# Three-operator kernel on one core: the mixer's second product in halves through the projections' bank, a later round for the second group, and another order at the end of the last batch

## The chip, the cores and the metric

The kernel runs on one core of a Trainium2 chip. The metric is the device time of one execution in microseconds (us), less is better. On the core, TensorE (PE) multiplies matrices, VectorE (DVE), ScalarE (ACT) and GpSimd (POOL) work on vectors, and SyncE (SP) issues the DMA transfers; each engine takes its instructions strictly in the order in which they stand in its own queue. TensorE writes into PSUM, a memory of 8 banks of 512 fp32 elements on each of 128 partitions.

## The reference, cut to what matters

Three operators follow one another on a batch of B = 4 sequences of S = 768 positions with 512 features. The third is the one whose second product the change touches.

```python
# 1: attention in chunks of 32 with a context of 16 to the left and 8 to the right (8 heads of 64)
a = softmax(scale * q_chunk @ k_context.T);  x = a @ v_context
# 2: causal attention with E = 4 experts as heads (width 64), two chosen per position
logits = x @ w_gate                     # the two best, softmax -> w
for e in range(E):
    a = softmax(causal(scale * (x @ wq[e]) @ (x @ wk[e]).T))
    out += w[e] * (a @ (x @ wv[e]) @ wo[e])
# 3: mixer along the positions (rank 32), then two layers (512 -> 2048 -> 512)
h = (x.transpose(0, 2, 1) @ U) @ V
u = x + h.transpose(0, 2, 1)
return u + np.maximum(u @ w_ch1, 0.0) @ w_ch2
```

## The kernel before

The program has two phases. In the first, each batch goes through twelve rounds; round r treats one pair of experts (`pr`, two pairs) and one block of 128 positions (`i`, six blocks), so that rounds 0 to 11 cover a batch. A round (`rnd`, line 700) writes down, in this order: the scores and softmax of its own block (`scores`), the chunk attention of a unit of the next batch (`local_scores`, `local_turn`), a list `fill1`, the transposes of the previous round's probabilities (`turn_scores`), a list `fill2`, and then, as one unbroken run on TensorE, the products with the values (`values`) and, where asked, the mixer's first product (`mix_down`). The lists carry the projections of later halves (`qk_proj`, `v_proj`) and the mixer's other steps. In the second phase TensorE runs the two layers over all batches (`ph` and `po`, lines 294 and 310, and `acc`, line 990).

A scheduler lays out each engine's queue from the written order, the dependencies and its own estimates, while the order of writing alone decides which buffer a tile gets. So a moved line can change the queues of whole batches. No table of order was written by hand; the rounds in which pieces stand are fixed in the loop of lines 821 to 861.

The names that matter below. `sc` is a block's scores in PSUM, `nmc` the negative maximum over a row (line 606, VectorE), `ac` the exponentials (line 591, ScalarE), `su` the sums and their reciprocals (lines 610 and 611, VectorE). Line 613 scales `ac` in place by `su` and the gate on GpSimd. `tpc` are the transposes of `ac` (line 631); line 634 copies them from PSUM to `ath`, in turn on ScalarE and VectorE. `t` takes the products (line 696), and line 649 copies a block of the result into `yT`, which holds 128 features by 768 positions of one pair. Once a pair has its six blocks, the mixer works on it: `mix_turn` transposes `yT` (`pyt`, line 659) and copies it to `y` (lines 661 and 662); `mix_down` multiplies by U (six small matmuls out of `y` and `u_s`, line 696); `mix_keep` sums the pieces into `qf` and `qm` (lines 673 to 679); `mix_up` multiplies by V (`pz`, line 687), adds `yT` (`z`, line 688, one VectorE instruction of 768 columns), and sends `z` to memory (`zs`, line 689), from where the second phase loads it (`zf`).

PSUM is shared by tags. `TC` has two buffers of two banks each, which `sc`, `tpc`, `pyt` and `pz` take in turn. `TQ` is one bank with one buffer; the projections `pqk` (line 499, 384 columns wide) and `pv` (line 539) live in it, in the last batch also the second layer's `po`. A tile can be written only when the one that held its buffer before has been read out.

`mix_up` of a batch's first pair stands at the head of `fill1` in round 0 of the next batch, that of the second pair in round 4. The last batch has no next one: after its twelve rounds comes an extra round that has no block of its own, with `mix_up(b, 0)` in its `fill1`, and then the second pair's `mix_turn`, `mix_down`, `mix_keep` and `mix_up`.

## Time and profile before

| what | us |
|---|---|
| three runs, least | 845.24 |
| three runs, median | 845.29 |
| three runs, most | 847.5 |
| the profiled execution, its own time | 846.73 |
| its span, from the first instruction to the last | 844.7 |
| TensorE busy in the span | 804.9 (95%) |
| VectorE busy | 625.0 (74%) |
| ScalarE busy | 498.0 (59%) |
| GpSimd busy | 155.8 (18%) |

Between the span and the execution's own time lie 2.03 us that no view shows. A busy TensorE means that a matmul was under way, not that it ran at its peak. A row of the timeline gives the start, the duration, the engine, the line, the operation and its operands, and in square brackets how long the engine sat idle before it and whose end released it; a row with xN merges N instructions that followed one another. A row of the stretches ("windows") gives the length, each engine's busy time, the clock that was granted to TensorE as a share of its full speed, and the DMA's share. Since queues are in order, an idle time in front of an instruction holds up all that stands behind it on the same engine.

### The profile page before, as it was taken

What the parts mean: (1) busy time and instruction counts of PE and PEld (TensorE: products, weight loads), DVE (VectorE), ACT (ScalarE), POOL (GpSimd) and SP (SyncE); (2) the same over time, 40 slices, a digit from 0 to 9 for tenths busy, and PEclk for the clock granted to TensorE, in tenths of its full rate; (3) what the DMA queues carried; (4) which work ended last, traced back from release to release, by engine and by line L of the source; (5) the groups of instructions that cost most, each with busy time, mean ns of one, the idle gap of its engine ahead of it and who ended that gap; (6) DMA issues with size and microseconds to landing.
All of it is one profiled execution on the core that took longest, in us unless ns stands there. A gap on an engine that the chain in (4) does not pass through costs nothing.

```text
span 844.7 us, 17957 instructions
## 1 busy us (share of the span) xinstructions
PE 804.9 (95%) x6396; PEld 721.1 (85%) x6396; DVE 625.0 (74%) x1990; ACT 498.0 (59%) x1464; POOL 155.8 (18%) x243
## 2 busy tenths in 40 slices
PE   7889999999998998889979999999999999999997
PEld 5768989889987897768767888899999999999996
DVE  4597768677767766899536999999769486684956
ACT  5688757667656755666424565666555464554642
POOL 1364344344333424223110000000000000000000
PEclk9999999999999999999979999999999999999999
DMA  9845323333313301263206744300303012030211
GB/s 289 256 137 155 100 81 104 91 123 109 94 54 95 95 2 45 87 191 104 75 19 204 222 155 163 101 26 1 125 1 126 1 45 81 1 125 2 76 50 51
DMA packets 38377, 81.54 MB, mean 97 GB/s; under 512 B 4368, under 2 KB 7952, under 8 KB 37520
## 3 DMA queue, kind: packets, MB, share of 16 engines
q1 hardware_dynamic: 38288, 80.39, 29.6%
q8 instruction: 51, 0.84, 0.4%
q14 instruction: 38, 0.31, 0.1%
HBM read 64.64 MB, written 15.73 MB: 95 GB/s over the span
## 4 chain that ended last, share of the span: by engine, by line
PE 71%; DMA 11%; DVE 10%; ACT 5%; issue 3%; SPq 0%; POOL 0%; DVEq 0%; ACTq 0%; POOLq 0%
PE acc L990 23%; PE ph L294 13%; PE t L696 8%; PE pqk L499 6%; DMA raw<-in_w 5%; PE tpc L631 3%; PE pv L539 3%; PE po L310 3%; PE s L440 3%; PE sc L579 3%; PE sc L580 2%; DMA part<-o 2%; PE tp L468 2%; ACT ac L591 1%; DMA k_t<-in_kw 1%
## 5 line engine op out<-in xcount | busy, mean ns | idle before, releaser
L990 PE MATMUL acc<-xhi,sw 128*128 128x256 f32 x1008 | 189.2, 283 | 0.4 <-ACT o L315 0.3
L990 PEld LDWEIGHTS acc<-xhi,sw 128*128 128x128 f32 x1008 | 159.7, 189 | 5.5 <-ACT o L315 0.5
L990 PE MATMUL acc<-xlo,sw 128*128 128x256 f32 x504 | 139.4, 283 | 0.2 <-DVE xlo L909 0.2
L905 DVE TENSOR_TENSOR sx<-t 128x256 f32<-128x256 f32 x180 | 68.1, 422 | 66.8 <-ACT t L898 66.8
L898 ACT ACTIVATE t<-ph 128x512 f32<-128x512 f32 x72 | 43.0, 598 | 99.0 <-PE ph L294 99.0
L613 POOL TENSOR_SCALAR ac<-ac,su,g 128x128 f32<-128x128 f32 (+5 forms) x96 | 71.4, 752 | 147.5 <-DVE su L611 95.2
L990 PEld LDWEIGHTS acc<-xlo,sw 128*128 128x128 f32 x504 | 95.6, 190 | 2.4 <-DVE xlo L909 0.4
L908 ACT CAST xhi<-sx 128x256 fp32r<-128x256 f32 x205 | 74.6, 406 | 21.8 <-DVE sx L905 18.9
L591 ACT ACTIVATE ac<-sc,nmc 128x128 f32<-128x128 f32 (+5 forms) x96 | 60.3, 632 | 38.3 <-DVE nmc L606 26.8
L909 DVE TENSOR_TENSOR xlo<-sx,xhi 128x256 fp32r<-128x256 f32 x205 | 77.5, 422 | 2.8 <-ACT xhi L908 2.0
L447 ACT ACTIVATE a<-a,nm 128x96 f32<-128x96 f32 x192 | 69.9, 368 | 12.7 <-DVE nm L444 12.2
L294 PE MATMUL ph<-zh,wp_l 128*128 128x512 f32 x192 | 61.0, 398 | 1.0 <-ACT zh L282 1.0
L294 PE MATMUL ph<-zh,wp_h 128*128 128x512 f32 x192 | 60.9, 394 | 0.0
L631 PE MATMUL tpc<-ident_s,ac 128*128 128x128 f32 x336 | 53.9, 281 | 6.5 <-ACT ath L634 2.8
L452 POOL TENSOR_TENSOR a<-a,rs 128x288 f32<-128x288 f32 x64 | 42.6, 667 | 91.8 <-DVE rs L451 32.9
L440 PE MATMUL s<-k_t,q_t 128*128 128x96 f32 x384 | 54.0, 275 | 4.3 <-DVE nm L444 1.6
L294 PE MATMUL ph<-zl,wp_h 128*128 128x512 f32 x176 | 56.1, 394 | 0.0
L440 PEld LDWEIGHTS s<-k_t,q_t 128*128 128x128 f32 x384 | 48.9, 192 | 7.7 <-DVE nm L444 3.6
L579 PE MATMUL sc<-kl,qs 128*128 128x384 f32 (+2 forms) x144 | 51.0, 355 | 3.8 <-DVE z L688 1.0
L444 DVE CUSTOM_DVE_ANT_0 a<-s,band_s 128x96 f32<-128x96 f32 x192 | 40.1, 251 | 16.8 <-PE s L440 14.3
L696 PE MATMUL t<-ath,vt 128*64 128x128 f32 x672 | 47.1, 280 | 4.3 <-DVE ath L634 3.7
L631 PEld LDWEIGHTS tpc<-ident_s,ac 128*128 128x128 f32 x336 | 39.9, 145 | 12.2 <-issue 4.6
(183 smaller groups left out, 1975.1 us busy)
## 6 DMA issues: line engine op xcount, KB each, us to landing
raw<-in_w SPq DMA_DIRECT2D x64, 256.0 KB, 3.5
q_t<-in_qT SPq DMA_DIRECT2D x32, 384.0 KB, 3.3
k_t<-in_kw SPq DMA_DIRECT2D x32, 288.0 KB, 3.8
v_t<-in_vw SPq DMA_DIRECT2D x32, 288.0 KB, 3.2
part<-o SPq DMA_DIRECT2D x24, 256.0 KB, 2.5
pt<-part SPq DMA_DIRECT2D x6, 1024.0 KB, 5.0
out<-pt SPq DMA_DIRECT2D x24, 256.0 KB, 2.3
zf<-zs SPq DMA_DIRECT2D x8, 512.0 KB, 4.5
```

Of the source, the lines that this page charges most:

```text
L294: nc.tensor.matmul(p, w[f // 4][:, pr, fs], z[:, pr], start=(n == 0), stop=(n == 5))
L440: last = nc.tensor.matmul(s[:, j, :], w["q"][:, qd * 3 + j], w["k"][:, qd * 3 + j], start=True, stop=True).ins
L447: nc.scalar.activation(a[:, j, :], a[:, j, :], AF.Exp, bias=nm[:, j:j + 1], scale=-1.0, accum_out=ss[:, j:j + 1])
L579: nc.tensor.matmul(s[:, o:o + w], q, kl[b, e, hf][:, :w], start=True, stop=False)
L591: nc.scalar.activation(aa[h][:, :n], src, AF.Exp, bias=nm[:, h:h + 1], scale=1.0, accum_out=su[:, h:h + 1])
L613: nc.gpsimd.tensor_scalar(aa[h][:, :n], aa[h][:, :n], su[:, h:h + 1], gates[b, i // 3][:, i % 3, 2 * pr + h:2 * pr + h + 1], op0=ALU.mult, ...
L631: nc.tensor.transpose(tp[h][:, j * 128:(j + 1) * 128], aa[h][:, j * 128:(j + 1) * 128], ident_s)
L696: session.append(nc.tensor.matmul(*a, **kw).ins)
L905: nc.vector.tensor_tensor(x, t[:, p[0], p[1]], t[:, q[0], q[1]], op=op)
L908: nc.scalar.copy(hi, x)
L909: nc.vector.tensor_sub(lo, x, f32(hi))
L990: ended[0] = nc.tensor.matmul(acc[n][:, m], w[:, ms], x, start=(f == FA and u == 0 and m == 0), stop=(f == NF - 2 and u == 2 and m == 1)).ins
```

## The change

Four things are changed.

- In five of the eight calls of `mix_up` (both pairs of batches 0 and 1 and the first pair of batch 2) the product goes through `TQ` in two halves: one matmul of 384 columns into the one bank, one add of 384 columns out of it, then the same for the other half. The three other calls keep the two banks of `TC` and the one add of 768 columns.
- The second pair's `mix_up` stands in round 5 of the next batch, not in round 4.
- In the last batch's extra round `mix_up(b, 0)` is taken out of `fill1` and stands behind the second pair's `mix_turn`.
- From round 10 of the last batch on, line 613's scalings are issued on VectorE, not on GpSimd. These are four instructions: two of 640 columns and two of 768.

```diff
--- before.py
+++ after.py
@@ -610,10 +610,12 @@
             nc.vector.tensor_scalar(su, su, 1e-9, None, op0=ALU.add)
             nc.vector.reciprocal(su, su)
             for h in range(2):
-                nc.gpsimd.tensor_scalar(aa[h][:, :n], aa[h][:, :n], su[:, h:h + 1],
-                                        gates[b, i // 3][:, i % 3, 2 * pr + h:2 * pr + h + 1], op0=ALU.mult, op1=ALU.mult)
+                (nc.vector if ending[0] else nc.gpsimd).tensor_scalar(
+                    aa[h][:, :n], aa[h][:, :n], su[:, h:h + 1], gates[b, i // 3][:, i % 3, 2 * pr + h:2 * pr + h + 1],
+                    op0=ALU.mult, op1=ALU.mult)
             a_ts[b, pr, i] = aa
 
+        ending = [False]
         ncp = [0]
         turned_ins = []
 
@@ -681,11 +683,18 @@
         def mix_up(b, pr):
             qm = qms.pop((b, pr))
             z = cw.tile([128, S], F32, name="z", tag="ac", bufs=NAC)
-            p = ps.tile([128, 1024], F32, name="pz", **TC)
-            for hf in range(2):
-                cs = slice(128 + hf * HALF, 128 + (hf + 1) * HALF)
-                nc.tensor.matmul(p[:, cs], qm, v_st[:, hf * HALF:(hf + 1) * HALF], start=True, stop=True)
-            nc.vector.tensor_add(z, p[:, 128:128 + S], yT[b, pr])
+            if b < B - 2 or (b, pr) == (B - 2, 0):
+                for hf in range(2):
+                    cs = slice(hf * HALF, (hf + 1) * HALF)
+                    p = ps.tile([128, 512], F32, name="pz", **(TQ))[:, :HALF]
+                    nc.tensor.matmul(p, qm, v_st[:, cs], start=True, stop=True)
+                    nc.vector.tensor_add(z[:, cs], p, yT[b, pr][:, cs])
+            else:
+                p = ps.tile([128, 1024], F32, name="pz", **TC)
+                for hf in range(2):
+                    cs = slice(128 + hf * HALF, 128 + (hf + 1) * HALF)
+                    nc.tensor.matmul(p[:, cs], qm, v_st[:, hf * HALF:(hf + 1) * HALF], start=True, stop=True)
+                nc.vector.tensor_add(z, p[:, 128:128 + S], yT[b, pr])
             nc.sync.dma_start(zs[b][:, pr, :], z)
 
         session = []
@@ -821,11 +830,12 @@
             work = pieces(b, 1) + ([] if last else pieces(b + 1, 0))
             for r, (pr, i) in enumerate(ROUNDS):
                 n = (FILL0 if b == 0 else FILL)[r] if work else 0
+                ending[0] = last and r >= 10
                 now, work = work[:n], work[n:]
                 f1, f2 = now[:1], now[1:]
                 if b and r == 1:
                     f2 = f2 + [lambda: mix_turn(b - 1, 1)]
-                if b and r == 4:
+                if b and r == 5:
                     f1 = [lambda: mix_up(b - 1, 1)] + f1
                 if r == 10:
                     f2 = f2 + [lambda: mix_turn(b, 0)]
@@ -851,8 +861,9 @@
                     if r == 5:
                         close_proj()
             if last:
-                rnd(None, old, fill1=[lambda: mix_up(b, 0)])
+                rnd(None, old)
                 mix_turn(b, 1)
+                mix_up(b, 0)
                 session.clear()
                 pq = ps.tile([128, 512], F32, name="pq", **TE)
                 mix_down(b, 1, pq)
```

How this moves instructions, at three places. The first is TensorE's queue at the start of batch 1 (round 0, after the mixer's first product for batch 0, `pq`); `tp` and `s` belong to the chunk attention. Before:

```order
L696 MATMUL pq<-y,u_s 32x128 x6
L468 MATMUL tp<-ident_s,a 96x128 x6
L499 MATMUL pqk<-xl,wqk_h 128x384 x4
L499 MATMUL pqk<-xh,wqk_h 128x384 x4
L499 MATMUL pqk<-xh,wqk_l 128x384 x4
L440 MATMUL s<-k_t,q_t 128x96 x3
L687 MATMUL pz<-v_st,qm 128x384 x2
L631 MATMUL tpc<-ident_s,ac 128x128 x6
L440 MATMUL s<-k_t,q_t 128x96 x3
L631 MATMUL tpc<-ident_s,ac 128x128 x6
```

Now, beginning at the same round's products with the values (the rows between, which stand behind the same `pq`, are twelve `tpc`, six `tp` and the next scores):

```order
L440 MATMUL s<-k_t,q_t 128x96 x3
L705 MATMUL t<-ath,vt 64x128 x12
L690 MATMUL pz<-v_st,qm 128x384
L633 MATMUL tpc<-ident_s,ac 128x128
L440 MATMUL s<-k_t,q_t 128x96 x3
L690 MATMUL pz<-v_st,qm 128x384
L661 MATMUL pyt<-ident_s,yT 128x128 x6
L633 MATMUL tpc<-ident_s,ac 128x128
L440 MATMUL s<-k_t,q_t 128x96 x3
L499 MATMUL pqk<-xl,wqk_h 128x384 x4
L499 MATMUL pqk<-xh,wqk_h 128x384 x4
L499 MATMUL pqk<-xh,wqk_l 128x384 x4
```

The group of twelve `pqk` that stood ahead of `pz` stands behind both halves of `pz` now, and the next scores and the transposes of `yT` (`pyt`) have come ahead of it; the pieces of projection behind it stand later too, about a round, through the batches 1 to 3.

The second place is TensorE's queue at the end of the last batch, from the last scores to the first product of the second phase (`ph`). Before:

```order
L582 MATMUL sc<-tri_s,identb_s 128x128
L631 MATMUL tpc<-ident_s,ac 128x128 x10
L696 MATMUL t<-ath,vt 64x128 x10
L696 MATMUL t<-y,u_s 32x128 x6
L687 MATMUL pz<-v_st,qm 128x384 x2
L631 MATMUL tpc<-ident_s,ac 128x128 x12
L659 MATMUL pyt<-ident_s,yT 128x128 x5
L696 MATMUL t<-ath,vt 64x128 x12
L659 MATMUL pyt<-ident_s,yT 128x128
L294 MATMUL ph<-zh,wp_l_5571 128x512 x2
```

Now:

```order
L582 MATMUL sc<-tri_s,identb_s 128x128
L633 MATMUL tpc<-ident_s,ac 128x128 x16
L705 MATMUL t<-ath,vt 64x128 x10
L705 MATMUL t<-y,u_s 32x128 x6
L633 MATMUL tpc<-ident_s,ac 128x128 x6
L661 MATMUL pyt<-ident_s,yT 128x128 x5
L705 MATMUL t<-ath,vt 64x128 x12
L696 MATMUL pz<-v_st,qm 128x384 x2
L661 MATMUL pyt<-ident_s,yT 128x128
L294 MATMUL ph<-zh,wp_l_5581 128x512 x2
```

Six of the twelve transposes of the last block have moved ahead of the products with the values, the other six ahead of `pyt`, and `pz` has moved from ahead of them to behind the last products; from the first `ph` on the queue reads as before. (The trace counts two matmuls for each of the products `t<-ath` and `t<-y` of these rows: x20 there is x10 here.)

The third is VectorE's queue over the same stretch, from the last maxima to the second copy of `y`. Before:

```order
L606 TENSOR_REDUCE nmc<-sc 128x1 x2
L610 TENSOR_SCALAR su<-su 128x2
L611 RECIPROCAL su<-su 128x2
L634 COPY ath<-tpc 128x640
L675 TENSOR_TENSOR qf<-t,qf 32x128
L678 CAST qm<-qf 32x128
L679 TENSOR_TENSOR qm<-qf,qm 32x128
L688 TENSOR_TENSOR z<-pz,yT 128x768
L634 COPY ath<-tpc 128x768
L662 COPY y<-pyt 128x256
```

Now, from the last sums on:

```order
L610 TENSOR_SCALAR su<-su 128x2
L611 RECIPROCAL su<-su 128x2
L613 TENSOR_SCALAR ac<-ac,su,g 128x768 x2
L636 COPY ath<-tpc 128x640
L677 TENSOR_TENSOR qf<-t,qf 32x128
L636 COPY ath<-tpc 128x768
L680 CAST qm<-qf 32x128
L681 TENSOR_TENSOR qm<-qf,qm 32x128
L697 TENSOR_TENSOR z<-pz,yT 128x768
L664 COPY y<-pyt 128x256
```

The two scalings of 768 columns have come in behind the sums, and `z` has moved behind the last copy `ath` and the steps of `qm`. The two scalings of 640 columns, not shown, stand one round earlier, ahead of the last maxima.

## Rows read from the trace of the kernel before

**Rows 1.** The stretches: length, busy PE, PEld, DVE, ACT, POOL, granted clock, DMA share, GB/s.

```profile
150.00:350.00 200.00, 191.26 (x1920) 174.38 (x1920) 142.79 (x525) 128.58 (x439) 75.75 (x120) 1.00 0.25 79
350.00:370.00 20.00, 14.65 (x96) 11.45 (x95) 18.11 (x61) 12.82 (x38) 4.44 (x8) 1.00 0.54 165
450.00:845.00 395.00, 388.50 (x2575) 355.94 (x2573) 308.48 (x808) 213.92 (x518) 0.00 (x0) 1.00 0.24 82
```

**Rows 2.** TensorE's waits in 150 to 340: in total, times, longest, in us.

```profile
PE t L696 <- DVE ath L634: 2.5, 5, 0.9
...
PE tpc L631 <- DVE z L688: 1.1, 2, 0.6
...
PE tpc L631 <- ACT ath L634: 0.8, 2, 0.4
PE sc L579 <- DVE z L688: 0.7, 2, 0.5
```

**Rows 3.** One line's instructions over the span: duration min/median/max in ns, starts, forms.

```profile
L687 PE MATMUL pz<-v_st,qm x16: 335/379/657, 150.2 to 445.9; 96*128 96x384 f32 x16
...
L688 DVE TENSOR_TENSOR z<-pz,yT x8: 936/955/958, 151.5 to 446.8; 128x768 f32<-128x768 f32 x8
...
L487 DVE TENSOR_TENSOR xl<-t,xh x32: 526/554/560, 18.5 to 319.4; 128x384 fp32r<-128x384 f32 x32
...
L130 DVE TENSOR_SCALAR d_t<-d_t x41: 258/290/503, 37.7 to 498.4; 128x256 uint32<-128x256 uint32 x40, 128x192 uint32<-128x192 uint32 x1
```

**Rows 4.** The stretch of one batch, instructions on `pqk` alone, then on `pv` alone.

```profile
241.00:329.00 88.00, 20.73 (x101) 17.28 (x102) 8.83 (x16) 7.64 (x16) 1.00 0.19 57
...
241.00:329.00 88.00, 10.35 (x72) 9.12 (x72) 0.93 (x6) 2.23 (x6) 1.00 0.19 57
```

**Rows 5.** TensorE's longest wait in 354 to 370.

```profile
PE t L696 <- DVE ath L634: 2.1, 1, 2.1
```

**Rows 6.** The timeline at the end of the first phase, rows left out between.

```profile
425.43 1.62 PE L631 MATMUL tpc<-ident_s,ac 128*128 128x128 f32 x10 [1.40 <-ACT ac L591]
...
426.40 0.17 DVE L611 RECIPROCAL su<-su 128x2 f32<-128x2 f32 x1
426.74 1.94 POOL L613 TENSOR_SCALAR ac<-ac,su,g 128x768 f32<-128x768 f32 x2 [3.58 <-DVE su L611]
427.08 0.82 DVE L634 COPY ath<-tpc 128x640 f32<-128x640 f32 x1 [0.52 <-PE tpc L631]
...
428.05 2.40 PE L696 MATMUL t<-ath,vt 128*64 128x128 f32 x20 [1.01 <-DVE ath L634]
...
433.45 0.98 PE L687 MATMUL pz<-v_st,qm 96*128 96x384 f32 x2 [1.57 <-DVE qm L679]
...
437.19 0.96 DVE L634 COPY ath<-tpc 128x768 f32<-128x768 f32 x1 [1.70 <-PE tpc L631]
...
438.20 1.53 PE L696 MATMUL t<-ath,vt 128*64 128x128 f32 x24 [0.25 <-DVE ath L634]
...
440.10 0.33 PE L659 MATMUL pyt<-ident_s,yT 128*128 128x128 f32 x1 [0.36 <-ACT yT L649]
```

**Rows 7.** Stretches around the end and one hole earlier, columns as in the first group.

```profile
427.00:438.00 11.00, 8.37 (x52) 6.83 (x51) 3.37 (x6) 1.51 (x4) 1.68 (x2) 0.53 0.10 37
428.00:437.00 9.00, 7.38 (x47) 6.12 (x48) 1.74 (x4) 1.51 (x4) 0.68 (x1) 0.50 0.08 32
355.00:356.00 1.00, 0.00 (x0) 0.00 (x0) 1.00 (x6) 0.84 (x4) 0.13 (x1) 1.00 0.00 0
```

**Rows 8.** TensorE's timeline at the start of batch 1, rows left out between.

```profile
144.19 1.27 PE L696 MATMUL t<-ath,vt 128*64 128x128 f32 x20
145.38 0.85 PE L696 MATMUL pq<-y,u_s 128*32 128x128 f32 x12
...
150.63 0.82 PE L631 MATMUL tpc<-ident_s,ac 128*128 128x128 f32 x6
...
156.74 1.53 PE L696 MATMUL t<-ath,vt 128*64 128x128 f32 x24
```

## The prediction

> **What bounds the kernel now.** I read the stretches first. TensorE is busy for 191.26 of the 200 us from 150 to 350, and for 388.50 of the 395 us of the second phase [rows 1]: in both it is the bound, and only its idle time can be won there. Two places stand out. From 350 to 370 it is busy for 14.65 of 20 us while VectorE is busy for 18.11 [rows 1], the longest wait being 2.1 us for a copy `ath` on VectorE [rows 5]. And at the end of the first phase it waits in a chain and runs at a lower clock: in the 11 us from 427 to 438 the mean granted clock is 0.53, in 428 to 437 it is 0.50, which is the level of 1.2 GHz instead of 2.4 [rows 7]. If the clock has these two levels, (1 - 0.53) / 0.5 x 11 = 10.3 us were spent at the lower one. The chain itself is in the timeline [rows 6]: the last scalings end on GpSimd at 428.68, yet the queue puts the first product `pz` ahead of the transposes of what they scale, `pz` waits for `qm` until 433.45, and only then come the transposes, the copy, the products at 438.20 and the last `pyt` at 440.10. The last wait of this chain is `pz`'s, not the scaling's.
>
> Next, TensorE's waits in the middle of the batches [rows 2]: behind `mix_up` it waited 1.1 + 0.7 = 1.8 us for `z` to give back one of the two big buffers, and 0.8 us for copies by ScalarE that were late for the same buffers. Against these stand 2.5 us of waits for copies by VectorE, which the change doesn't aim at.
>
> **The first mixer edit, halves.** It removes the big buffer from five calls. The waits that can go are those 1.8 + 0.8 = 2.6 us; none need go if the next `tpc` is late for another reason, so 0 to 2.6. I take 2.6, as `z` or the copies that shared its buffers are named as the releaser in each of them.
>
> It adds a wait. Both halves go through one bank, so the second matmul waits until the first half's add has read it. A matmul takes 0.38 us, an add of 384 columns 0.55 (the row of line 487 has this shape), one of 768 columns 0.955 [rows 3]. The cycle until the bank is free is thus 0.93 us plus what the add waits in VectorE's queue. In the new queue only one transpose, or one and three small score products, stand between the halves. A transpose is 0.82 / 6 = 0.14 us [rows 8]. So between nothing (the scheduler's neighbours fill it) and 0.9 per call; I take 0.4, the middle, and 2.0 for five calls, with 0 to 4.5 for the range. Behind the second `pz` in TensorE's queue stand transposes and then the twelve `pqk`, and all wait with it.
>
> Two adds of 384 cost VectorE 2 x 0.554 = 1.11 us instead of 0.955 [rows 3], 0.15 more a call, 0.8 in all. VectorE is busy for 142.79 of 200 us there [rows 1], so this lies in its idle time; where a copy `ath` stands right behind, it costs up to 0.15 each. I take nothing.
>
> The row shows the fixed part of 0.15 us that an instruction pays whatever its width. The Trainium skill, "VectorE: DVE Perf Modes", section "The TRN2 errata — SBUF-src ops pay a fixed extra latency per instruction", says that many small tiles pay a fixed cost each and advises wide ones, which speaks against splitting the add. This trace agrees, with 0.15 us. With all five on the path the sum would be 0.8 worse.
>
> **What the queues do with it.** The new use of the bank moves the pieces of projection about a round later through batches 1 to 3, since the projections take the same single bank. No work is added by that, so in batches 1 and 2, where TensorE is the bound, it gives nothing on balance: some waits close, others open. I take 0 with 2.5 either way, as large as the waits for `ath` [rows 2]. The later round for the second pair's `mix_up` costs and gains nothing by itself: no engine wants its `z` within the batch, only the transfer to memory, whose queue (SP) has nothing behind it there that is due.
>
> In batch 3 the moved pieces can fall into the hole of 20 - 14.65 = 5.35 us [rows 1]. But VectorE is the late one there, and two `pqk` bring it 2 x 8.83 / 8 = 2.2 us of evictions [rows 4]. So from -4 (they fill the hole) to +2.2 (they lengthen VectorE's line); I take 0, since work moves, but none goes away.
>
> **The end.** Here the rows carry a sum. The sums `su` end at 426.57, and GpSimd begins at 426.74 and needs 1.94 for both halves [rows 6]. On VectorE one scaling of 768 columns takes between 0.55 and 0.955. The upper end is the one-element pace of the 768-wide add. The lower comes from a scalar operation of the same kind out of and into SBUF, 0.29 us for 256 columns: with the fixed 0.15 that is 0.54 ns a column, half of the add's (0.955 - 0.554) / 384 = 1.04, and 0.15 + 768 x 0.53 gives 0.55 [rows 3]. I take 0.55, the same kind of instruction. The transposes of the previous block end at 427.05. Those of the last block's first expert then begin at 426.57 + 0.55 = 427.1, end at 427.95; the second scaling ends at 427.7 and the copy `ath` of 640 columns (0.82), which stands behind it on VectorE now, at 428.5 instead of 427.90. That is what the scalings cost: the first products begin 0.5 later than before. At full clock they take 1.27, the mixer's first product 0.85, six transposes 0.82, five `pyt` 0.7, the last products 1.53 [rows 8]. So: products to 429.8, mixer to 430.6, second expert's transposes to 431.4, `pyt` to 432.1. The copy of 768 (0.96) begins at 431.5, ends at 432.5, the last products run from 432.6 to 434.1. The steps of `qm` on VectorE follow that copy and end around 433.1, beside the products. `pz` takes two matmuls, 0.5, and the last `pyt` ends at 435.1 at the latest, against 440.43 before: -5.3. With the slow scaling price 0.8 less, -4.5. What then stands behind, `ph`, has the same queue as before, and in the second phase TensorE is the bound, so this carries through to the end. The two scalings of 640 columns come earlier, ahead of the last maxima, in a stretch in which VectorE is idle before those maxima; I take them as free.
>
> Some 3 of the 5.3 us are the clock and not the order: the waits that made TensorE idle for 1.01 and 1.57 us [rows 6] go, and with them, I expect, most of the stretch at 1.2 GHz.
>
> **Sum.** -2.6 + 2.0 + 0 + 0 - 5.3 = -5.9. Against the profiled execution's own 846.73 that gives 840.8, against the runs' median of 845.29 it gives 839.4. The profile was longer than the median by 1.44, and a stretch of low clock of another length would explain that, in which case the median has less to win. I take 840.0, which puts the kernel before at 845.9 by this reckoning. By the bounds alone the sum runs from -14 to +5, but they don't all fall on one side.
>
> **Rivals.**
> The clock falls all the same. Before it fell TensorE had been idle for 1.40, transposed for 1.62, and been idle for 1.01 us [rows 6]; the 1.40 stays, since the exponentials release the transposes. Against it: around 355 TensorE stood still for a whole microsecond, 2.1 in all, at a granted clock of 1.00 [rows 5, 7]. If it falls in the same place for the same 10 us, the new chain takes about twice the prices above until the clock rises near 437.6: transposes to 428.7, products (2.40 [rows 6]) to 431.1, mixer to 432.8, transposes to 434.4, `pyt` to 435.8, the last products begin there and end near 438.3, `pz` and `pyt` around 439. That is a gain of 1.5: 845.9 - 0.6 - 1.5 = 843.8. The Trainium skill, "TensorE: Matmul & The Clock Gate", section "HAM oscillation — how this bites in real kernels", says that idle gaps between short bursts of matmuls bring the clock down again each time. The fall at 427 is of this sort, the hole at 355 speaks against it.
>
> The halves stall more than I think, 0.9 a call: 2.5 worse, 842.5.
>
> The moved pieces fill batch 3's hole: 4 better, 836.0.
>
> The projections' bank becomes the bound, and the kernel gets slower. A half then holds the bank for 0.38 + 0.55 us and about 0.4 of waiting for VectorE (waits there average 2.5 / 5 = 0.5 [rows 2]), 1.35 each and 2.7 a call, and the projections behind wait for all of it: 5 x 2.7 = 13.5, less 2.6 and 5.3, is +5.6, or 851.5. It decides where the bank has less than two calls' 5.4 us of free time in a batch. The instructions on `pqk` and `pv` take 20.73 + 8.83 + 7.64 + 10.35 + 0.93 + 2.23 = 50.7 of 88 us, counted one after the other [rows 4], which leaves 37 less what evictions wait; so this is unlikely.
>
> **Chances.** The forecast, with a short fall of the clock among it (up to 842), 0.52; the clock falls as before (843.8) 0.15; the halves stall (842.5) 0.10; the hole filled (836.0) 0.10; the bank bound (851.5) 0.08; mixtures 0.05. The range of 836.5 to 844.2 leaves out the last rival and the far end of the filled hole. A measurement tells some 0.3% from no change, 2.5 us, so faster means under 842.8 and slower over 847.8. Faster: 0.52 + 0.10 + half of the stalls + some of the mixtures = 0.70; slower 0.08; the rest, 0.22, is the same.
>
> **What would show it.** Right: behind `pz` no wait of TensorE for `z` in batches 1 and 2; the two 768-wide scalings on VectorE at 0.55 each; the last `pyt` some 5 us earlier relative to the last scores; a granted clock of 1.00 in most of that stretch. Wrong: a second `pz` that waits near a microsecond, `pqk` waiting for a half's add, scalings at 0.95, a clock of 0.50 for ten microseconds, or a second phase that gives the gain back in waits for `zh` or weights.

## Result and the profile after

The changed kernel takes 840.32 us (median of ten runs, 837.64 to 844.53). In the same comparison the kernel before takes 847.38 (845.24 to 850.35), 2.1 more than the median of the three runs known ahead. The ratio is 0.9909, interval 0.9888 to 0.9931: 0.9% faster. The forecast was 840.0 in a range of 836.5 to 844.2.

The profiled execution has a span of 838.5 us against 844.7. Its first line of busy times:

```profile
PE 803.5 (96%) x6396; PEld 720.8 (86%) x6396; DVE 631.1 (75%) x1999; ACT 497.5 (59%) x1464; POOL 152.7 (18%) x239
```

TensorE is busy for nearly as long as before (804.9) in a shorter span: idle time went, not work.

To see where, the span is cut at four points that every version has in the same order on TensorE: the mixer's first product (`y` by U) of batch 0's first pair, that of batch 2's first pair, the last scores `sc`, and the first `ph` behind the last `pyt`. Of the kernel before, the three stretches between them (the columns are length, then busy PE, PEld, DVE, ACT, POOL, granted clock, DMA share, GB/s):

```profile
145.38:327.37 181.99, 173.93 (x1768) 158.74 (x1767) 128.74 (x490) 118.38 (x407) 69.49 (x110) 1.00 0.27 82
327.37:423.79 96.42, 89.20 (x623) 74.36 (x621) 76.88 (x202) 55.38 (x148) 25.90 (x34) 1.00 0.32 105
423.79:440.18 16.39, 11.65 (x88) 9.36 (x88) 5.13 (x10) 4.34 (x10) 1.94 (x2) 0.69 0.07 25
```

And of the changed kernel:

```profile
147.68:322.85 175.17, 170.12 (x1756) 156.18 (x1754) 128.09 (x491) 117.28 (x405) 69.71 (x108) 1.00 0.28 85
322.85:422.13 99.28, 93.01 (x636) 77.68 (x634) 81.87 (x208) 55.96 (x150) 24.65 (x34) 0.98 0.31 102
422.13:433.07 10.94, 8.02 (x88) 6.32 (x88) 5.34 (x11) 4.31 (x10) 0.00 (x0) 1.00 0.01 1
```

The length less the busy PE is TensorE's idle time: 8.06, 7.22 and 4.74 us before, 5.05, 6.27 and 2.92 after. The first two stretches belong together, since the change moves projections from the first into the second (busy 173.93 to 170.12, 89.20 to 93.01). The differences of the traces, then: up to the first point +2.30 (147.68 - 145.38, work that the change doesn't touch), the middle 274.45 - 278.41 = -3.96, the end 10.94 - 16.39 = -5.45, the second phase (838.5 - 433.07) - (844.7 - 440.18) = +0.91. Sum -6.20, the difference of the spans. Of the +2.30, TensorE's busy time makes 1.89 (132.77 to 134.66 us, 1304 matmuls in both), with the clock low for 3.4 us between 40 and 50 us, where it was 1.00 before; its waits there for loads of `k_t` were shorter, 0.9 instead of 1.5.

The end of the changed kernel, rows left out between, to be read against [rows 6]:

```profile
423.67 1.65 PE L633 MATMUL tpc<-ident_s,ac 128*128 128x128 f32 x10 [1.31 <-ACT ac L591]
...
425.00 1.27 DVE L613 TENSOR_SCALAR ac<-ac,su,g 128x768 f32<-128x768 f32 x2
...
425.83 0.85 PE L633 MATMUL tpc<-ident_s,ac 128*128 128x128 f32 x6 [0.52 <-DVE ac L613]
426.19 0.82 DVE L636 COPY ath<-tpc 128x640 f32<-128x640 f32 x1
...
427.06 1.31 PE L705 MATMUL t<-ath,vt 128*64 128x128 f32 x20 [0.39 <-DVE ath L636]
...
429.08 0.88 PE L633 MATMUL tpc<-ident_s,ac 128*128 128x128 f32 x6
...
431.10 1.53 PE L705 MATMUL t<-ath,vt 128*64 128x128 f32 x24 [0.60 <-DVE ath L636]
...
432.56 0.62 PE L696 MATMUL pz<-v_st,qm 96*128 96x384 f32 x2
...
433.02 0.30 PE L661 MATMUL pyt<-ident_s,yT 128*128 128x128 f32 x1
```

The idle times in the brackets are 1.31, 0.52, 0.39 and 0.60, where they were 1.40, 1.01, 1.57 and two smaller ones; `pz` doesn't wait any more, and no matmul has the doubled price of [rows 6]. The granted clock of this stretch is 1.00 (third row of the table), where it was 0.69.

In the middle, TensorE's longest waits from the first point to the mixer's product of batch 2's second pair (in total, times, longest):

```profile
PE s L440 <- DVE nm L444: 1.7, 2, 1.0
PE pv L539 <- DVE lg L542: 1.6, 1, 1.6
PE sc L579 <- DVE ath L636: 0.9, 1, 0.9
PE t L705 <- DVE ath L636: 0.8, 4, 0.3
```

No wait of a matmul for `z` is left, and none of `pz`. The longest in total, 1.7 us, was 0.2 before: the chunk attention's scores `s`, which stand between the two halves of the second pairs' `pz` (round 5), wait 0.73 and 0.98 us for VectorE, which is late with the maxima (`nm`) of earlier ones. The second of the two:

```profile
276.81 0.91 PE L440 MATMUL s<-k_t,q_t 128*128 128x96 f32 x6 [0.98 <-DVE nm L444]
```

The adds of 384 columns, and the scalings on VectorE (lines 691 and 613; duration min/median/max in ns):

```profile
L691 DVE TENSOR_TENSOR z<-pz,yT x10: 528/546/557, 154.0 to 329.9; 128x384 f32<-128x384 f32 x10
```

```profile
L613 DVE TENSOR_SCALAR ac<-ac,su,g x4: 607/644/678, 419.6 to 425.6; 128x640 f32<-128x640 f32 x2, 128x768 f32<-128x768 f32 x2
```

One thing is worse than in the profile before. In batch 3, where that one had its hole around 355, the clock falls now:

```profile
350.00:360.00 10.00, 7.42 (x60) 5.88 (x59) 8.80 (x33) 5.78 (x19) 2.95 (x4) 0.90 0.28 93
360.00:370.00 10.00, 10.00 (x58) 8.70 (x57) 9.17 (x26) 6.12 (x15) 1.00 (x1) 0.93 0.33 107
```

(0.10 + 0.07) x 10 / 0.5 = 3.4 us at 1.2 GHz. Ahead of it TensorE stood still for 2.58 us, `pz` of batch 2's second pair waiting for a big buffer that held scores:

```profile
357.19 0.62 PE L696 MATMUL pz<-v_st,qm 96*128 96x384 f32 x2 [2.58 <-ACT ac L591]
```

This fall does not belong to the change alone. In three of the five other profiles that have the old middle (the end alone, the order alone and the first trial with extra matmuls, all below) the clock falls in batch 3 as well, about 40 us behind the second point, where TensorE waits 1.8 to 2.7 us for a copy by ScalarE. In the first trial with extra matmuls:

```profile
370.00:380.00 10.00, 10.00 (x47) 8.22 (x48) 8.48 (x22) 6.30 (x19) 2.13 (x3) 0.83 0.43 141
```

Over the whole profile TensorE worked for 10.2 us at the low clock before, all at the end of the first phase, and for 6.8 us now: these 3.4 and the 3.4 between 40 and 50 us.

### The profile page after: what moved, and what is told of

Same layout as the page of the kernel before. It is cut to its first block, busy times and chain, and to the rows that moved or that the text cites. A ratio compares the mean times of both kernels' runs of the same rounds, so it can differ in the third digit from the quotient of the medians.

```text
span 838.5 us, 17962 instructions
## 1 busy us (share of the span) xinstructions
PE 803.5 (96%) x6396; PEld 720.8 (86%) x6396; DVE 631.1 (75%) x1999; ACT 497.5 (59%) x1464; POOL 152.7 (18%) x239
## 4 chain that ended last, share of the span: by engine, by line
PE 70%; DVE 12%; DMA 11%; ACT 4%; issue 3%; SPq 1%; POOL 0%; DVEq 0%; ACTq 0%; POOLq 0%
PE acc L1001 22%; PE ph L294 13%; PE t L705 7%; PE pqk L499 7%; DMA raw<-in_w 4%; PE s L440 3%; PE pv L539 3%; PE tpc L633 3%; PE sc L579 3%; PE po L310 2%; PE sc L580 2%; PE tp L468 2%; DMA part<-o 1%; DMA zf<-zs 1%; DMA raw<-in_wqk 1%
## 5 line engine op out<-in xcount | busy, mean ns | idle before, releaser
L613 POOL TENSOR_SCALAR ac<-ac,su,g 128x128 f32<-128x128 f32 (+5 forms) x92 | 67.6, 743 | 155.5 <-DVE su L611 57.9
L606 DVE TENSOR_REDUCE nmc<-sc 128x1 f32<-128x512 f32 (+2 forms) x48 | 39.0, 818 | 12.9 <-PE sc L582 12.4
```

Of the source, the lines that this page charges most:

```text
L613: (nc.vector if ending[0] else nc.gpsimd).tensor_scalar(aa[h][:, :n], aa[h][:, :n], su[:, h:h + 1], gates[b, i // 3][:, i % 3, 2 * pr + h: ...
```

## Experiments

Each was timed in five rounds beside the kernel before, whose median was 847.5 to 847.8 throughout.

### The end alone, and the middle alone

The end alone leaves out the halves and the later round (edit on the changed kernel):

```diff
-            if b < B - 2 or (b, pr) == (B - 2, 0):
+            if False:
...
-                if b and r == 5:
+                if b and r == 4:
                     f1 = [lambda: mix_up(b - 1, 1)] + f1
```

> Only the end is changed (the last batch's mix_up behind the second transposes, and the four scalings on VectorE); all eight mix_up stay in the two-bank buffers and the second pair's in round 4. The queues up to the last scores are those of the kernel before. Theory (the end's chain was bound by pz and the low clock): 5 to 5.5 us less than the kernel before, the last pyt 5.3 us earlier behind the last scores, no stretch of ten us at clock 0.50. Rival (the middle carries the gain, the end only moves a stall into the second phase): 0 to 2 us less.

Measured: 842.72 us, ratio 0.9941 (0.9917 to 0.9965), 5.0 us by the ratio. From the last scores to the first `ph` 10.95 us, as in the whole change. The theory holds.

The middle alone puts the end back (edit on the changed kernel):

```diff
-                ending[0] = last and r >= 10
+                ending[0] = False
...
-                rnd(None, old)
+                rnd(None, old, fill1=[lambda: mix_up(b, 0)])
                 mix_turn(b, 1)
-                mix_up(b, 0)
```

> Only the middle is changed (five mix_up in halves through the projections' bank, the second pair's in round 5); the end is that of the kernel before. Theory: 0.6 us less by the forecast's sum, 1.7 us less by the changed kernel's trace, whose last scores end at 422.36 against 424.02. Rival (halves stall on the one bank): 1 to 5 us more than the kernel before.

Measured: 844.00 us, ratio 0.9955 (0.9932 to 0.9978), 3.8 us less (1.9 to 5.8 by the interval). Neither the forecast's 0.6, or the 1.7 by the trace, nor the rival: the middle is worth about six times what the sum gave it. Its two stretches:

```profile
146.13:321.40 175.27, 170.14 (x1756) 156.22 (x1754) 128.07 (x491) 117.27 (x405) 69.79 (x109) 1.00 0.28 85
321.40:421.62 100.22, 93.39 (x636) 77.30 (x634) 81.16 (x206) 55.86 (x150) 25.65 (x36) 0.98 0.30 101
```

The idle times are 5.13 and 6.83, as in the whole change but for 0.6 us in batch 3. The two halves of the change add up to 5.0 + 3.8 = 8.8, against 7.7 by the whole change's ratio, which the intervals don't tell apart.

### Which half of the end: the order or the engine

Only the scalings on VectorE, everything else as before (edit on the kernel before):

```diff
-                nc.gpsimd.tensor_scalar(aa[h][:, :n], ...
+                (nc.vector if ending[0] else nc.gpsimd).tensor_scalar(aa[h][:, :n], ...
...
+        ending = [False]
...
+                ending[0] = last and r >= 10
```

> Only the four scalings of the last rounds go to VectorE; everything else, TensorE's queue too, is that of the kernel before. Theory (the chain at the end is set by pz's wait for qm and by its place ahead of the transposes): no gain, 0 to 0.5 us more, since the copy of 640 columns comes later behind the scalings. Rival (the slow GpSimd is what held the end): 1.5 to 3 us less.

Measured: 848.30 us, ratio 1.0003 (0.9982 to 1.0025): no gain. The products with the values wait longer, 1.84 instead of 1.01 us, for the copy that stands behind the scalings, and the stretch of the end, at the same low clock, is 17.10 instead of 16.39:

```profile
430.30 2.40 PE L705 MATMUL t<-ath,vt 128*64 128x128 f32 x20 [1.84 <-DVE ath L636]
```

```profile
425.27:442.37 17.10, 11.53 (x89) 9.27 (x88) 6.30 (x12) 4.31 (x10) 0.00 (x0) 0.70 0.06 24
```

Only the order, the scalings on GpSimd (edit on the kernel before):

```diff
-                rnd(None, old, fill1=[lambda: mix_up(b, 0)])
+                rnd(None, old)
                 mix_turn(b, 1)
+                mix_up(b, 0)
```

> Only the order at the end is changed (mix_up of the last batch's first pair behind the second transposes); the scalings stay on GpSimd. TensorE's queue is that of the run with the whole end changed. Theory (the order is what counts): nearly the whole gain of the end, 4.5 to 5 us less than the kernel before, with the first transposes of the last block waiting some 0.6 us for GpSimd. Rival (the scaling's engine is what counts, 1.94 us on GpSimd in two instructions): 0 to 2 us less, since the products with the values now stand behind transposes that wait for GpSimd.

Measured: 844.08 us, ratio 0.9961 (0.9934 to 0.9987), 3.3 us less; the expected 4.5 to 5 lie inside the interval. The transposes wait 0.73 us for GpSimd, as expected, and yet the stretch of the end takes 10.79 us, 0.16 less than with VectorE, because the copy of 640 columns, which no longer stands behind the scalings, comes earlier (3.29 us behind the last scores instead of 4.06):

```profile
432.74 0.87 PE L633 MATMUL tpc<-ident_s,ac 128*128 128x128 f32 x6 [0.73 <-POOL ac L613]
```

```profile
428.76:439.55 10.79, 7.92 (x88) 6.32 (x88) 4.17 (x9) 4.34 (x10) 1.94 (x2) 1.00 0.01 2
```

So the order carries the end: without it nothing was gained, with it alone the stretch is as short as with both. The runs of the two (842.72 and 844.08) have overlapping intervals and don't tell the engines apart.

### How much of the end is the clock

To hold the clock up in the old order, extra matmuls whose result nothing uses fill the gaps. First trial, on the kernel before:

```diff
+        def spin(t, n, after):
+            for _ in range(n):
+                m = nc.tensor.matmul(t[:, 128:256], ident_s, ident_s, start=True, stop=True).ins
...
+                hold['spun'] = spin(t, 10, hold['sc'])
...
+                hold['spun'] = spin(t, 7, hold['tr'])
...
+                    hold['spun'] = spin(t, 10, session[-1])
```

> The kernel before, with 27 extra matmuls of 128 columns on TensorE in the three gaps of the end (10 behind the last scores, 7 behind the transposes of the last block but one, 10 behind the mixer's first product); their result is not used, and every other queue is as before. They fill the idle times of 1.40, 1.01 and 1.57 us. Theory (half of the end's gain is the clock, half the order): the clock stays at 1.00, and from the last scores to the first ph it takes 13 us instead of 16.4, so about 3 us less than the kernel before, against 10.9 us with the new order. Rival (the low clock lay only under waits and cost nothing): 16 us as before, same time or slower.

Measured: 848.68 us, ratio 1.0025 (0.9999 to 1.0051). The trial failed by its size: a matmul took 0.245 us, twice what I had planned with, and the last ten, in the tile that the copies to `qf` read, held those copies up, so that `pz` waited 1.56 us behind them all the same. The clock was 1.00 in the whole stretch, and yet it took 16.87 us:

```profile
435.81 2.50 PE L706 MATMUL t<-ident_s 128*128 128x128 f32 x20
439.86 0.59 PE L689 MATMUL pz<-v_st,qm 96*128 96x384 f32 x2 [1.56 <-DVE qm L681]
```

Second trial, 5 and 4 matmuls in the first two gaps, none in the third:

```diff
-                hold['spun'] = spin(t, 10, hold['sc'])
+                hold['spun'] = spin(t, 5, hold['sc'])
...
-                hold['spun'] = spin(t, 7, hold['tr'])
+                hold['spun'] = spin(t, 4, hold['tr'])
...
-                    hold['spun'] = spin(t, 10, session[-1])
```

> The kernel before with nine extra matmuls of 128 columns at the end, 5 behind the last scores and 4 behind the transposes of the last block but one, sized by the first trial's 0.245 us each so that they fit into the idle 1.40 and 1.01 us; none behind the mixer's first product, where they had held up the copies out of the same tile. Theory (about half of the end's gain is the clock): no low clock in the end, 12.5 to 13.5 us from the last scores to the first ph instead of 16.4, so 2.5 to 3.5 us less than the kernel before. Rival (the idle 1.57 us in front of pz brings the clock down in any case): 15 to 16.5 us, 0 to 1 us less.

```profile
423.98 1.33 PE L704 MATMUL t<-ident_s 128*128 128x128 f32 x10
...
427.00 1.06 PE L704 MATMUL t<-ident_s 128*128 128x128 f32 x8
...
431.83 0.59 PE L689 MATMUL pz<-v_st,qm 96*128 96x384 f32 x2 [1.56 <-DVE qm L681]
```

```profile
423.91:437.51 13.60, 10.12 (x107) 8.45 (x106) 5.13 (x10) 4.34 (x10) 1.94 (x2) 1.00 0.08 30
```

In the trace the theory holds: clock 1.00, and the old order takes 13.60 us instead of 16.39, with the wait of 1.56 us in front of `pz` still there. The run with the halves alone (below) had the old end at clock 1.00 without any extra matmul, and takes 13.60 there too. So at full clock the order is worth 13.60 - 10.95 = 2.65 us, and the clock was worth 2.79 in the profile of before.

The timed runs don't show the 2.79: 847.79 us, ratio 1.0008 (0.9983 to 1.0033), which leaves a gain of 1.4 us at most. Two records bear on this. First, 2.79 is the most that any profile shows: in the four with the old end and the scalings on GpSimd the stretch takes 16.39, 14.58, 14.51 and 13.60 us at mean clocks of 0.69, 0.88, 0.88 and 1.00, so the clock cost 2.79, 1.0, 0.9 and nothing. Nor is the new order free of it. In one of its seven profiles, that with six calls in halves (below), the end ran at a mean clock of 0.86 and took 12.10 us instead of 10.94:

```profile
430.00:440.00 10.00, 9.40 (x84) 7.79 (x83) 3.93 (x8) 2.58 (x7) 0.00 (x0) 0.84 0.01 2
```

Second, the mean clock over the whole span is on record for every timed run. Of the second trial's twelve, the profiled one is the only one at 1.000; they average 0.9943, the twelve with the end alone 0.9942, the 89 of the kernel before 0.9921. These means don't say where the clock was low, and they take in the last 5 us, behind TensorE's last matmul. Taken as they are, the fillings and the new end each save some 3.5 us at the low clock ((0.9942 - 0.9921) x 845 / 0.5), which is 1.8 us of time at most; yet the runs with the new end are 5.0 us faster and those with the fillings are not. So in the timed runs the order is the larger part of the end, and the clock is an estimated 2 us at most.

### Which half of the middle: the halves or the later round

Only the halves, the second pair in round 4, the end as before (edit on the middle alone):

```diff
-                if b and r == 5:
+                if b and r == 4:
                     f1 = [lambda: mix_up(b - 1, 1)] + f1
```

> Only the first edit: five mix_up in halves through the projections' bank, the second pair's still in round 4, the end as before. Theory (halves give back the big buffers and let the projections come later, and the round does little): most of the middle's gain, 2.5 to 4 us less than the kernel before, TensorE's idle time from the first mixer product to the last scores 12 us instead of 15.3. Rival (the halves need the later round, in round 4 they hold up the projections): 0 to 1.5 us less, with waits of pz or pqk for z.

Measured: 843.81 us, ratio 0.9964 (0.9941 to 0.9986), 3.1 us less. The stretches:

```profile
146.66:320.89 174.23, 170.29 (x1756) 155.94 (x1754) 126.61 (x491) 117.51 (x405) 69.71 (x109) 1.00 0.28 85
320.89:419.83 98.94, 92.45 (x635) 76.31 (x634) 80.52 (x206) 56.57 (x150) 25.66 (x36) 1.00 0.31 102
419.83:433.43 13.60, 8.06 (x89) 6.40 (x88) 5.12 (x10) 4.34 (x10) 1.95 (x2) 1.00 0.08 30
```

Idle 3.94 and 6.49, together 10.43: 4.85 less than before, more than both edits together. The theory holds, the rival falls.

Only the later round, all eight products in the big buffers, the end as before (edit on the middle alone):

```diff
-            if b < B - 2 or (b, pr) == (B - 2, 0):
+            if False:
```

> Only the second edit: the second pair's mix_up in round 5, all eight in the big buffers, the end as before. Theory: within 0.3% of the kernel before, 1 us less at most. Rival (the round is what gives the middle's gain): 2 to 4 us less.

Measured: 844.47 us, ratio 0.9969 (0.9952 to 0.9986), 2.6 us less. Here the theory falls:

```profile
150.27:328.85 178.58, 173.79 (x1769) 158.41 (x1767) 129.55 (x490) 118.11 (x407) 69.70 (x110) 1.00 0.28 83
328.85:426.67 97.82, 90.80 (x624) 75.41 (x622) 77.08 (x202) 54.81 (x148) 23.79 (x34) 0.98 0.31 103
```

Idle 4.79 and 7.02, together 11.81: 3.47 less than before. Alone, the later round wins in batches 1 and 2 nearly what the halves win (8.06 to 4.79 and to 3.94). Together they don't add up (5.05). In round 4 the second pair's `pz` had taken a big buffer between scores and transposes that both wanted it; either edit takes it out of there. That much is in the waits: those of `sc` for `z` and of `tpc` for copies by ScalarE [rows 2] are gone, those of the first pairs' round stay (up to the product of batch 2's second pair):

```profile
PE t L705 <- DVE ath L636: 2.3, 4, 1.2
PE tpc L633 <- DVE z L697: 1.1, 2, 0.6
```

The views of the stretch up to batch 2's first pair name most of the 3.3 us: besides these two (0.7 and 0.8), the products wait 0.8 us for copies by VectorE instead of 2.1, and the chunk attention's transposes `tp` 0.4 us for ScalarE instead of 1.3; against that stands a new wait of `tpc` of 0.6 us for which the view names no releaser. Whether the buffer or the changed order of the queues closed the waits of the products and of `tp` is not shown.

### Two attempts to do better

A sixth call in halves, against the 2.58 us in batch 3:

```diff
-            if b < B - 2 or (b, pr) == (B - 2, 0):
+            if b < B - 1:
```

> The changed kernel with a sixth call in halves, that of batch 2's second pair, whose pz waited 2.58 us for a big buffer held by scores in batch 3 (357.19). Theory (that wait is for the buffer): the wait of pz goes and the clock doesn't fall around 357, 1 to 3 us less than the changed kernel, 837 to 839. Rival (VectorE is the late one there, busy 8.8 of 10 us, and the wait moves to the next instruction): the same as the changed kernel, 839 to 841.5.

Measured: 844.00 us, ratio 0.9958 (0.9937 to 0.9979), 3.7 us more than the changed kernel's median, and the intervals of the two ratios lie apart. The wait moved, as the rival said, and came twice:

```profile
357.88 0.42 PE L633 MATMUL tpc<-ident_s,ac 128*128 128x128 f32 x2 [2.47 <-DVE d_t L131]
...
366.78 0.41 PE L690 MATMUL pz<-v_st,qm 96*128 96x384 f32 x1 [2.12 <-DVE qs L519]
```

Transposes wait 2.47 us behind VectorE's decoding of weights (line 131), and `pz`, now in the bank of the projections, 2.12 us for VectorE to read out a `pqk` (line 519). It is VectorE that is late there, whichever buffer is used.

The changed kernel without the later round:

```diff
-                if b and r == 5:
+                if b and r == 4:
                     f1 = [lambda: mix_up(b - 1, 1)] + f1
```

> The changed kernel with the second pair's mix_up put back into round 4: halves and the new end, without the later round. Theory (the later round costs about 1 us once the halves are there, TensorE's idle time in batches 1 and 2 was 3.9 us without it and 5.0 with it, 8.1 before): 1 us less than the changed kernel, 838 to 840. Rival (the runs' scatter hides it or batch 3's hole takes it back): the same as the changed kernel.

The changed kernel once more beside it, without an edit:

> The changed kernel once more, beside the others on the same chip. Every theory: 0.9% less than the kernel before, as in its first runs.

And the version without the later round, with the scalings on GpSimd as well:

```diff
-                ending[0] = last and r >= 10
+                ending[0] = False
```

> Halves and the new order at the end, the second pair in round 4 and the scalings left on GpSimd. Theory (the engine of the scalings counts for little): within 0.5 us of the same kernel with the scalings on VectorE. Rival (it is worth what the two runs of the end alone differed by): 1.4 us more.

Measured: 837.24 us, ratio 0.9895 (0.9858 to 0.9932) without the later round; 839.97, ratio 0.9908 (0.9876 to 0.9940), for the changed kernel again; 838.98, ratio 0.9901 (0.9865 to 0.9938) with GpSimd. The first lies below the second as expected, but the intervals of all three overlap, so the runs show no difference among them. The trace of the first:

```profile
146.72:321.67 174.95, 171.11 (x1757) 156.62 (x1755) 127.07 (x492) 117.47 (x406) 70.22 (x110) 1.00 0.28 85
321.67:421.30 99.63, 93.03 (x636) 76.80 (x634) 80.52 (x206) 56.37 (x150) 23.60 (x33) 0.99 0.30 101
```

```profile
350.00:360.00 10.00, 8.32 (x61) 6.59 (x58) 8.88 (x32) 4.66 (x15) 2.07 (x2) 1.00 0.33 119
360.00:370.00 10.00, 10.00 (x60) 8.06 (x59) 9.59 (x28) 7.51 (x20) 4.07 (x6) 1.00 0.46 142
```

Idle 3.84 and 6.60: in the middle the trace bears the expectation out. But its second phase takes 407.05 us (839.3 - 432.25), 405.43 and 405.63 in the two profiles of the changed kernel, so there the gain is given back. Around 357 the clock falls in all four profiles that have halves and the later round, and in none of the three that have halves without it. But in batch 3 it falls also in four profiles without halves, three of them without the later round, and in the profile shown here it fell at another place (0.83 from 320 to 330). That the later round brings it down is not shown.

## Why the prediction was right or wrong

The time came out within 0.4 us, partly by luck: the three runs known ahead lay low, so that the starting point of 845.9 was 1.5 us under the median of the ten, and the gain was undersized by about as much, 5.9 us against a measured 7.1 by the medians, 7.7 by the ratio. The end was forecast right; the middle was forecast at 0.6 and is worth 3.8 by its own run.

**What bounds the kernel.** Right. TensorE's busy time stayed, the idle time went, and the end's chain was `pz`'s place and wait, not the scaling: with the scalings alone moved nothing was gained, with the order alone 3.3 us of the end's 5.0, which their intervals don't tell apart.

**The end, -5.3.** Right, -5.45 in the profile, 5.0 by the runs with the end alone. From the first transposes to the end of the last `pyt` the forecast had 435.1 - 425.43 = 9.7 us, the trace has 433.32 - 423.67 = 9.65. A scaling of 768 columns took 0.676 us, not 0.55: with 0.610 at 640 columns (the means of the two forms) that is 0.52 ns a column, the double pace that I took, with a fixed part near 0.28 instead of 0.15. The Trainium skill, "VectorE: DVE Perf Modes", section "The perf-mode tier table (the rule you actually need)", puts an fp32 `tensor_scalar` out of SBUF at twice the one-element pace; the slope agrees. The transposes of the last block began 0.5 us later than forecast, only 0.1 of it by the longer scaling, the rest by sums that ended 0.1 later and by the gaps before and behind the scaling; the steps behind made it up, most of all `pz` and the last `pyt`, for which the forecast had left room.

**Three of these from the clock.** Right for the profile of before (2.79), which is the largest fall of any with that end; in the timed runs it is an estimated 2 us at most. The rival that the clock falls anyway did not come true in the changed kernel's two profiles, but it did at the new end with six calls in halves. The evidence that I had set against it was weak: 2.1 us of standing still had left the clock up in batch 3 [rows 5, 7], yet in other profiles of the same middle it fell some 10 us further on, and in the changed kernel behind 2.58 us. No length of a single wait separates the cases, for with the later round alone it fell behind 0.80 us. The Trainium skill, "TensorE: Matmul & The Clock Gate", section "HAM oscillation — how this bites in real kernels", says, of waits for transfers, that idle gaps bring the clock down again; the runs agree in so far as the falls named here stand behind waits, but the waits of the old end left it at 1.00 in the run with the halves alone.

**The waits on `z`, -2.6.** Right for `z`: no matmul waits for it any more. Of the 0.8 for ScalarE's copies 0.3 is left, and `sc` now waits 0.5 for such copies.

**The new wait of the halves, +2.0.** This step failed. I took the middle between nothing and 0.9 us a call. Measured: no matmul of a second half waits for the first half's add in any of the five calls (one weight load does, 0.27 us). The scheduler put other work (`tpc`, and `s` or products) between the halves. In the two calls in round 5 it is this work that waits, `s` for 0.73 and 0.98 us, which the forecast didn't name. As for the price of splitting on VectorE, it is 2 x 0.546 - 0.955 = 0.14 us a call; 0.15 was forecast.

**The queues, 0, and batch 3's hole, 0.** Both undersized. With the halves alone the idle time of batches 1 and 2 fell by 4.1 us, 1.5 more than the named waits, so freeing the buffers and letting the projections come later closed more waits than it opened (one of them that of `tp` for ScalarE, 1.3 us before). In batch 3 the idle time fell by 0.95, inside the range that I gave, but by no more than 0.3 to 0.4 in the other two profiles of the same middle (6.83 and 6.93 us).

**The later round "costs and gains nothing by itself".** Wrong. Alone it wins 2.6 us; on top of the halves it costs 1.1 us more idle time in batches 1 and 2 (3.94 to 5.05, and 3.84 in the last version), in the profiles, not measurably in the runs. The wait that goes with it is that of `s` between the halves, 1.7 us in every profile with halves in round 5 and absent in those with halves in round 4. I had asked who wants its `z`, and not who wants the buffer that its `pz` holds in round 4.

**The rival on the other side**, the projections' bank as the bound, did not come: in the stretch of the waits above, `pqk` waits 0.7 us in all for the bank to be read out.

## What to carry to other kernels

In this kernel a product that shared large PSUM buffers with a chain of other tiles cost more by the order in which the buffers came free than by its own time; moving it to a small bank or to another round won much the same waits, and one of the two was enough. At the end of a phase look at which step of the chain waits last and move the others ahead of it before making any of them faster. Where a stretch runs at the low clock in one profile, find a profile of the same stretch at the full clock (here by filling its gaps with idle matmuls, or by chance) to see what the order is worth; and before the clock's part is carried over to the timed runs, look at the clock that these were granted.

## What was not expected of the hardware

Executions of one program differ by up to 10 us (842.80 to 852.83 for the kernel before in its last series of 19). Much of it goes with the clock: of the 89 runs of the kernel before, those at a mean clock of 0.989 or less have a median of 849.6 us, those from 0.990 to 0.992 one of 847.7, from 0.993 to 0.995 one of 846.3, and from 0.996 on one of 844.9.

The profiles show where. One place is the start: up to the first mixer product they took 144.54 to 150.27 us. The shortest (the second trial with extra matmuls) has the clock at 1.00 and no wait of TensorE for the loads of `k_t`, the longest (the later round alone) has both a low clock and such a wait:

```profile
0.00:60.00 60.00, 50.81 (x429) 40.52 (x430) 39.34 (x211) 41.30 (x159) 22.30 (x41) 1.00 0.78 232
```

```profile
0.00:60.00 60.00, 49.77 (x399) 40.86 (x400) 34.53 (x181) 36.69 (x137) 18.18 (x34) 0.91 0.76 219
```

```profile
PE s L440 <- DMA k_t<-in_kw: 2.6, 1, 2.6
```

Other places are batch 3 and the end of the first phase, 13.60 to 16.39 us for one order of instructions. The second phase, 403.35 to 407.05 us long over all versions, is a further part that I have not traced. Stretches cut at the same instructions, by contrast, agree within 0.1 us from profile to profile where neither a load nor the clock comes in: the first two stretches of batch 1 took 31.54 to 31.56 and 63.61 to 63.63 us in six profiles with the old middle.
